# Sigmoid attention and mixture of depths: choosing rows by scatters into zeroed tables in place of selection matmuls

## Chip, cores, metric
One core of a Trainium2 chip, one launch. The metric is the device time in microseconds, here the median of three runs. All times below are in us unless marked ns.

## What is computed
An attention with a sigmoid in place of a softmax over 8 sequences, 12 heads, 448 tokens of 64 values. Its output, laid out as 8 x 448 x 768, goes into a mixture of depths: each token has a score (its dot product with w_gate); in each sequence the 128 tokens with the highest score pass through a two-layer network with a gated residual, all others are copied.

```
scores = (q @ k.T) / sqrt(64) - log(448)
x      = (sigmoid(scores) @ v)            # -> (B, S, H*64)
gate   = x @ w_gate                        # (B, S)
out    = x.copy()
for b in range(B):
    top = argpartition(-gate[b], 128)[:128]
    y   = relu(x[b, top] @ w1) @ w2        # 768 -> 1024 -> 768
    out[b, top] = x[b, top] + sigmoid(gate[b, top])[:, None] * y
```

## The kernel before
**Steps and slots.** Two quads of four heads make a step `s` (0 to 11), and a step has seven slots `n`. In each slot PE makes the scores of one 64-key piece for both quads (`score`, L339), ACT squashes them (`squash`, L353), and PE multiplies earlier pieces with v (`value`, L368). All attention matmuls use 32x64 tiles of the PE array. The value matmuls run behind the scores: those of step `s` begin in slot 4 of step `s` and end in slot 3 of step `s+1`. After slot 3 DVE takes the finished outputs out of PSUM (`takes`, four transposes at L389, into `x_b`), the loads and transposes of the next quads follow (`turn`), and the scores of the mixture's gate are made (`gates`, L397 to L431). Program order is written out by hand; each engine runs its own instructions in that order.

**PSUM.** Eight banks: `PA[0]` and `PA[1]` have two banks each, filled by `score` and emptied by `squash`; `PO[x][pr]` are four single banks, which hold the outputs of quad `x` and are emptied by `take`.

**Blocks.** From step 4 on, slot 3 is followed by a block (`block`, L680): a list of 128x128 matmul groups of the mixture, `BLOCKS[s]`. An entry `(1, p, key)` is a partial product of the first layer for the pair of sequences `p` (`first`, 24 recorded matmuls of 128 columns, L560), `(2, p, key)` of the second layer (`second`, 8 of 384 columns, L624); each pair needs seven of either kind. `("t", b)` transposes the chosen rows of sequence `b` (`turn_rows`, L524), which ACT then copies out (L526, L527), and for the second sequence of a pair DVE makes three or four differences (L533, L543). `("c", b)` chooses rows. `places` in `block` gives each entry its PSUM bank. The steps whose values precede a block (`LATE`, from the first block's step to 10) use a slot order of their own (`first_slots`, `last_slot`, `LOW`, `HIGH`), in which the outputs of quad 0 are finished before the last scores; the others use `rounds`, and the step just before `LATE` ends with a slot (`split`) in which the values of both quads finish after the scores.

**Choosing rows.** When a sequence is complete its gate scores go to DRAM and come back spread over all partitions (`spread`, L437, tile `rep`). `ranking(b)` compares every token with all others on DVE, 16 passes of 448 elements (L445, L448), and sums to each token's rank in `above + level`. `place` compares the ranks with 0..127 (`hot`, L460); for sequences 2 to 5 it also multiplies `hot` with the tokens' number and score and adds over the four columns (L469, L473). `choose` sums over the partitions with matmuls on PE: four for sequences 0, 1, 6, 7 (L486), two for 2 to 5 (L482). `fetch` turns the result into a row index (L493) and copies the score (L496), and `gather` (L506) brings the 128 rows from `out` with an indirect DMA on POOL's queue. The mixture's result is added to these rows by DVE (L635) and scattered back (`scatter`, L644, also on POOL's queue).

**Queues.** SP issues nearly all loads and stores, in order, among them the stores of `x_b` (L406), the loads of `qT`, `raw_k` and the weights; ACT issues the loads of v (`load_v`, L153) from step 5 on; POOL issues the gate scores (L425), `spread`, gathers and scatters.

Of the kernel before, what the change touches and what calls it, by code (L numbers as in the profile page):

```python
# [17 lines left out]
def kernel(  # L18
# [114 lines left out]
    def load_v(s):  # L133


        if s >= NS:
            return
        if s in (1, 3):
            t = moe.tile([P, 6 * KH * P], F32, name="rows_t")[:, :4 * NU * Dh]
        else:  # L140
            t = vals.tile([P, 4 * NU * Dh], F32, name="raw_v")
        raw_v[s] = t = t.rearrange("p (h c) -> p h c", h=4)

        def block(x, r, n):
            return bass.AP(tensor=v.tensor,
                           offset=v.offset + (8 * s + 4 * x) * S * Dh + r * Dh,
                           ap=[[TB * Dh, TT], [S * Dh, 4], [1, n * Dh]])

        for m in range(4):
            y, odd = divmod(m, 2)  # L150
            rows = slice(m * TT, (m + 1) * TT)
            if s:
                (nc.scalar if s > 4 else nc.sync).dma_start(  # L153
                    out=t[rows], in_=block(y, odd * NU, NU))
            else:
                nc.sync.dma_start(out=t[rows, :, :NA * Dh], in_=block(y, odd * NA, NA))
                nc.sync.dma_start(out=t[rows, :, NA * Dh:],
                                  in_=block(1 - y, 2 * NA + 2 * odd, 2))
# [102 lines left out]
    earlier = const.tile([P, NC, S], mybir.dt.uint8, name="earlier")  # L261

    who = [const.tile([P, NC, 2], F32, name=f"who{x}") for x in range(2)]
    slots = const.tile([P, CAP], F32, name="slots")
    above = const.tile([P, NC], F32, name="above")
    level = const.tile([P, NC], F32, name="level")
    gate_s = const.tile([P, TT], F32, name="gate_s")
    place_s = const.tile([P, NC], F32, name="place_s")
    ones = const.tile([P, 1], F32, name="ones")

    def constants():
        make_identity(nc, iden)
        for a in range(4):
            p = slice(a * TT, (a + 1) * TT)
            nc.sync.dma_start(
                out=wg_b[p],
                in_=bass.AP(tensor=moe_w_gate.tensor, offset=moe_w_gate.offset + a * TT,
                            ap=[[0, TT], [P, HP], [1, TT]]))
        nc.gpsimd.iota(slots, pattern=[[1, CAP]], base=0, channel_multiplier=0,
                       allow_small_or_imprecise_dtypes=True)  # L280

        nc.gpsimd.memset(above, float(S))
        nc.gpsimd.memset(level, 0.0)
        nc.gpsimd.memset(ones, 1.0)
# [94 lines left out]
    def takes(s, x):  # L379
        for pr in range(2):  # L380
            take(s, pr, x)
# [70 lines left out]
    def added(b):  # L452

        return 1 < b < B - 2

    def place(b):

        nc.vector.tensor_add(place_s, above, level)
# [5 lines left out]
        if not added(b):  # L464
            return

        st[b]["sums"] = both = moe.tile([P, 2, P], F32, name="sums2")
        for x in range(2):
            nc.vector.tensor_scalar(out=both[:, x, :CAP], in0=st[b]["hot"][:, 0, :CAP],  # L469
                                    scalar1=who[b % 2][:, 0, x:x + 1], scalar2=None,  # L470
                                    op0=ALU.mult)
            for c in range(1, NC):
                nc.vector.scalar_tensor_tensor(  # L473
                    out=both[:, x, :CAP], in0=st[b]["hot"][:, c, :CAP],
                    scalar=who[b % 2][:, c, x:x + 1], in1=both[:, x, :CAP],
                    op0=ALU.mult, op1=ALU.add)

    def choose(b, ps):

        if added(b):  # L480
            for x in range(2):
                nc.tensor.matmul(ps[:CAP, x:x + 1], st[b]["sums"][:, x, :CAP], ones,  # L482
                                 start=True, stop=True)
        else:
            for c in range(NC):
                nc.tensor.matmul(ps[:CAP, :2], st[b]["hot"][:, c, :CAP], who[b % 2][:, c, :],  # L486
                                 start=(c == 0), stop=(c == NC - 1))
        return b, ps

    def fetch(b, ps):  # L490
        n = CAP
        idx = moe.tile([P, 1], I32, name="idx", bufs=5)
        nc.vector.tensor_scalar(out=idx[:n], in0=ps[:n, 0:1], scalar1=float(b * S),  # L493
                                scalar2=None, op0=ALU.add)
        got = moe.tile([P, 1], F32, name="got", bufs=4)
        nc.vector.tensor_copy(got[:n], ps[:n, 1:2])  # L496
# [4 lines left out]
        st[b].update(idx=idx, xe=xe, picked=got)  # L501
        gather(b)

    def gather(b):
        n = CAP
        nc.gpsimd.indirect_dma_start(  # L506
            out=st[b]["xe"][:n], out_offset=None, in_=rows_to(b),
            in_offset=bass.IndirectOffsetOnAxis(ap=st[b]["idx"][:n, 0:1], axis=0))
# [133 lines left out]
    def scatter(b):  # L642
# [5 lines left out]


    BLOCKS = {  # L650
# [8 lines left out]
    }  # L659

    LENT = {(7, 4): [(1, 6, 2)], (8, 4): [(1, 7, 0), (1, 5, 1)],
# [17 lines left out]

    def block(s):  # L680

        places = [PA[1][:, 0], PO[0][0], PO[0][1], PA[0][:, 0], PO[1][0], PO[1][1], PA[0][:, 0]]
        work = BLOCKS.get(s, ())
        if work and work[0][0] == "c":
            chosen = choose(work[0][1], places.pop(0))
        takes(s - 1, 0)
        if work and work[0][0] == "c":
            fetch(*chosen)
            work = work[1:]
        takes(s - 1, 1)  # L690
        stores(s, NF)
        if s in FULL[::2]:
            gates(2 * s - 2)
        for item in work:
            if item[0] == "t":
                turn_rows(item[1], [places.pop(0) for _ in range(2)])
                if item[1] == 0:
                    load_v(s)
            elif item[0] == "c":
                fetch(*choose(item[1], places.pop(0)))  # L700
            else:
                finish(item, begin(item, places.pop(0)))

# [211 lines left out]
    def after(s, n):  # L915

        if n == NF and s:
            odd = s in FULL[1::2]
            if s > 5:
                load_v(s)  # L920
            elif s < 4:
                load_v(s + 1)
# [44 lines left out]
                ranking(b)  # L967
        if n != NF:
            stores(s, n)

    RANKED = [(3, 1), None, (6, 1), (7, 6), (9, 1), (10, 6), (11, 6)]

    first_outs = ExitStack()

    def stream():
# [14 lines left out]
        constants()  # L990
        for s in range(NS):
            for n in range(NU):
                if n == 0 and s:
# [39 lines left out]
```

## Time and profile before
Median 446.51 of three runs (446.19 to 446.96).

| what | value |
|---|---|
| profiled execution | 446.79, span 445.0, granted PE clock 0.997 |
| attention scores L339 | 2624 records, 242.4 busy, 537 ns each, eight tiles at a time |
| attention values L368 | 2176 + 448 + 64 records, 536 to 544 ns each |
| first layer L560 / second layer L624 | 672 records of about 276 ns / 224 records of about 487 ns |
| choose L486, L482 | 32 records of 240 to 250 ns, 16 records of 255 ns |
| DVE: hot L460 | 8, 692 ns each |
| DVE: sums L469, L473 | 8 of 284 ns, 24 of 352 ns |
| DVE: ranking L445, L448 | 64 passes, 671 to 684 ns each |
| POOL: indirect DMA | 16, about 1.0 each to issue |
| POOL: other DMA | 15, about 0.58 each to issue |

How to read it: busy times of one engine overlap, since matmuls are pipelined and lie on different parts of the array, so the mean of one matmul is longer than the distance to the next. "Idle before" names what an engine waited for. The chain that ended last shows which work set the end. A timeline row gives the start, the length, the engine, the line, output and inputs, a count where several are merged, and in brackets how long the engine had been idle and what released it.

### The profile page before, as it was taken

The numbers are of one execution on the slowest core, as the hardware profiler recorded it, in microseconds if no ns is written. First come the engines' busy times: TensorE is split into PE (matmuls) and PEld (weight loads), VectorE is DVE, ScalarE is ACT, GpSimd is POOL, SyncE is SP. The second block draws the span as 40 slices with busy tenths as digits, with TensorE's granted clock in tenths as the row PEclk, the third lists the DMA queues.
The fourth block names the chain that finished last, engine by engine and source line by source line (L and its number), as shares of the span: only waits on it lengthen the run. The fifth ranks groups of instructions, "written<-read, shape, count | busy, mean of one in ns | idle before, by whom it ended". The sixth has DMA issues, their size and how long they took to land.

```text
span 445.0 us, 14349 instructions
## 1 busy us (share of the span) xinstructions
PE 430.2 (97%) x6374; PEld 259.2 (58%) x6374; DVE 302.6 (68%) x639; ACT 191.2 (43%) x257; POOL 32.8 (7%) x55
## 2 busy tenths in 40 slices
PE   7999999999999999999999999999999999999994
PEld 3456554444457568455447559546545749769952
DVE  4316368964958986966997885835796669883462
ACT  4666666666654633641660670552363330101100
POOL 7000000000001000100002000010000101001001
PEclk9999999999999999999999999999999999999998
DMA  8984835999645997699656598499945964611001
GB/s 234 246 249 110 300 87 114 212 186 232 200 143 120 233 308 186 181 234 298 219 181 177 154 234 147 138 224 241 269 167 107 190 219 63 119 36 72 1 0 71
DMA packets 112846, 76.80 MB, mean 173 GB/s; under 512 B 90304, under 2 KB 99136, under 8 KB 112784
## 3 DMA queue, kind: packets, MB, share of 16 engines
q1 hardware_dynamic: 106768, 61.55, 53.7%
q0 software_dynamic: 1984, 7.91, 6.2%
q10 hardware_dynamic: 4032, 6.42, 6.1%
q8 instruction: 50, 0.82, 0.8%
q14 instruction: 12, 0.10, 0.1%
HBM read 55.41 MB, written 20.46 MB: 170 GB/s over the span
## 4 chain that ended last, share of the span: by engine, by line
PE 88%; DVE 5%; ACT 3%; issue 1%; DMA 1%; POOLq 0%; ACTq 0%; DVEq 0%
PE a L339 27%; PE o L368 25%; PE o L624 12%; PE o L560 10%; PE a L560 7%; PE a L624 4%; ACT attn L353 2%; PE p L989 1%; DVE spare L208 1%; PE p L339 1%; DMA out_dram<-xe,idx 1%; ACT hidden L353 1%; DVE scr L448 1%; DVE scr L445 1%; DVE scr L397 1%
## 5 line engine op out<-in xcount | busy, mean ns | idle before, releaser
L339 PE MATMUL a<-qT,kT 32*64 32x448 f32 x2624 | 242.4, 537 | 0.6 <-DVE got L496 0.5
L353 ACT ACTIVATE attn<-a,bias_s 128x896 f32<-128x896 f32 x162 | 161.4, 1007 | 83.8 <-PE a L339 79.8
L368 PE MATMUL o<-attn,raw_v 32*64 32x448 f32 x2176 | 194.6, 536 | 0.5 <-issue 0.4
L339 PEld LDWEIGHTS a<-qT,kT 32*64 32x64 f32 x2624 | 92.8, 131 | 87.1 <-ACT attn L353 49.2
L368 PEld LDWEIGHTS o<-attn,raw_v 32*64 32x64 f32 x2176 | 74.3, 131 | 35.0 <-issue 26.9
L389 DVE STREAM_TRANSPOSE x_b<-o 128x448 f32<-128x448 f32 x48 | 27.8, 623 | 46.7 <-PE o L368 26.8
L368 PE MATMUL o<-attn,rows_t 32*64 32x448 f32 x448 | 42.3, 537 | 0.2 <-issue 0.2
L576 ACT ACTIVATE hidden<-hidden 128x512 f32<-128x512 f32 x12 | 7.5, 630 | 68.5 <-DVE hidden L573 68.5
L400 DVE TENSOR_REDUCE gate_p<-scr 128x14 f32<-128x448 f32 x48 | 29.8, 622 | 1.7
L321 DVE STREAM_TRANSPOSE kT<-raw_k 128x448 f32<-128x448 f32 x42 | 24.1, 613 | 8.8 <-DMA raw_k<-in_k_dram 7.6
L397 DVE TENSOR_TENSOR scr<-x_b,wg_b 128x448 f32<-128x448 f32 x48 | 29.4, 612 | 1.1
L573 DVE TENSOR_TENSOR hidden<-o,hidden 128x512 f32<-128x512 f32 x20 | 13.3, 688 | 21.1 <-PE o L560 20.9
L624 PE MATMUL o<-w_sb,hidden 128*128 128x384 f32 x80 | 27.4, 487 | 0.0
L635 DVE SCALAR_TENSOR_TENSOR xe<-o,gate,xe 128x384 f32<-128x384 f32 x36 | 20.5, 612 | 9.5 <-PE o L624 9.3
L313 DVE STREAM_TRANSPOSE qT<-qT 128x896 f32<-128x896 f32 x23 | 25.0, 1085 | 2.1 <-DMA qT<-in_q_dram 1.9
L448 DVE SCALAR_TENSOR_TENSOR scr<-rep,who,earlier 128x448 f32<-128x448 f32 (+1 forms) x32 | 21.8, 683 | 1.4
L560 PE MATMUL o<-rows_t,w_sb 128*128 128x128 f32 x192 | 22.7, 275 | 0.0
L560 PEld LDWEIGHTS o<-rows_t,w_sb 128*128 128x128 f32 x192 | 22.2, 192 | 0.3
L526 ACT ACTIVATE rows_t<-o 128x384 f32<-128x384 f32 x7 | 3.4, 484 | 43.9 <-PE o L524 43.9
L445 DVE TENSOR_SCALAR_CACHE_REDUCE scr<-rep,who 128x448 f32<-128x448 f32 (+1 forms) x32 | 21.5, 673 | 1.0
L368 PEld LDWEIGHTS o<-attn,rows_t 32*64 32x64 f32 x448 | 17.6, 131 | 6.4 <-issue 4.7
L624 PEld LDWEIGHTS o<-w_sb,hidden 128*128 128x128 f32 x80 | 14.7, 190 | 8.8
(114 smaller groups left out, 398.1 us busy)
## 6 DMA issues: line engine op xcount, KB each, us to landing
qT<-in_q_dram SPq DMA_DIRECT2D x24, 448.0 KB, 6.0
out_dram<-x_b SPq DMA_DIRECT2D x32, 336.0 KB, 8.8
raw_k<-in_k_dram SPq DMA_DIRECT2D x22, 448.0 KB, 5.1
spare<-sum SPq DMA_DIRECT2D x18, 384.0 KB, 5.7
raw_v<-in_v_dram ACTq DMA_DIRECT2D x28, 224.0 KB, 6.1
sum<-spare SPq DMA_DIRECT2D x8, 768.0 KB, 8.3
w_sb<-in_moe_w_dram SPq DMA_DIRECT2D x6, 768.0 KB, 7.1
rows_t<-in_v_dram SPq DMA_DIRECT2D x8, 224.0 KB, 5.1
```

The lines of the kernel that those rows point to most:

```text
L313: nc.vector.transpose(heads["q", i], heads["q", i])
L321: nc.vector.transpose(kt[:, e], t[:, e].rearrange("p (a n) d -> p n a d", a=2))
L339: nc.tensor.matmul(out[y * Dh:(y + 1) * Dh, h % 2, :S], kt[d, e, r:r + 2].rearrange("d r t -> d (r t)"), qt[d, e], start=(e == 0), stop=(e ...
L353: nc.scalar.activation(a, psc[:, :, :S], AF.Sigmoid, bias=bias_s, scale=QK_SCALE)
L368: nc.tensor.matmul(PO[x][pr][j * Dh:(j + 1) * Dh, :S], raw_v[s][rows, 2 * pr + j, at:at + Dh], attn[s, pr, n][rows, j, :], start=((s, x, p ...
L389: nc.vector.transpose(x_tiles[b][:, :, 2 * g + pr, :], PO[x][pr][:, :S].rearrange("p (r t) -> p r t", t=TT))
L397: nc.vector.tensor_tensor(out=tmp, in0=x_tiles[b][:, :, hp, :], in1=wg_b[:, hp:hp + 1, :].to_broadcast([P, TB, TT]), op=ALU.mult)
L400: nc.vector.tensor_reduce(out=gate_parts[b][:, :, hp], in_=tmp, axis=AX.X, op=ALU.add)
L445: nc.vector.tensor_scalar(out=junk[:n], in0=rep[:n], scalar1=own, scalar2=0.0, op0=ALU.is_gt, op1=ALU.add, accum_out=above[:n, c:c + 1])
L448: nc.vector.scalar_tensor_tensor(out=junk[:n], in0=rep[:n], scalar=own, in1=earlier[:n, c, :], op0=ALU.is_equal, op1=ALU.mult, accum_out=l ...
L560: nc.tensor.matmul(ps[:, f, :n], w((t * FH + f) * P, P), x[:, t, :n], start=(t == 0), stop=(t == KH - 1))
L624: nc.tensor.matmul(ps[:n, :DH], h[:, t, :n], w(t * DH, DH), start=(t == 0), stop=(t == FH - 1))
```

## The change
- For sequences 0 to 5 `choose` goes. Four tables per sequence in DRAM (448 rows of 2 floats each; 24 tables) have their first 128 rows set to zero at the start by 24 DMAs on POOL's queue, from a zeroed tile. `place` scatters, for each of the four columns of tokens, the pair (number, score) to the row that is the token's rank (four indirect DMAs), then loads the first 128 rows of each table (four DMAs). Each rank below 128 is found in one of the four tables, and zero in the others; `fetch` adds the four on DVE (a reduction) and makes the index. Sequences 6 and 7 keep the matmuls; the sums at L469 and L473 and the tile `ones` go.
- `fetch` moves out of the blocks, to slots named in `FETCHED`.
- The block of step 4 goes (it held only `("c", 0)`), so `LATE` begins with step 5, and step 4 has the order of steps 1 to 3. The transposes `("t", b)` of sequences 1 to 4 move: t1 from the end of block 5 to the front of block 6, t2 from the end of block 7 to its second place, t3 from the end of block 8 to the front of block 9, t4 from the end of block 10 to its second place, t5 stays at the end of block 11.
- `places` begins with the low banks `PO[0]` in place of `PA[1]`.
- `load_v(5)` moves from ACT's queue to SP's, `load_v(6)` and `load_v(9)` go behind the transposes in their block. `ranking` of sequences 3 and 5 comes one slot earlier.

```diff
-                (nc.scalar if s > 4 else nc.sync).dma_start(
+                (nc.scalar if s > 5 else nc.sync).dma_start(
...
+    tables = [[dram.tile([S, 2], F32, name=f"table{b}_{c}", bufs=1) for c in range(NC)]
+              for b in range(B - 2)]
...
+        for t in sum(tables, []):
+            nc.gpsimd.dma_start(out=t[:CAP].rearrange("i x -> (i x)"), in_=zero[0:1, :2 * CAP])
...
     def place(b):
+        if b < B - 2:
+            rank_of = moe.tile([P, NC], I32, name="rank_of")
+            nc.vector.tensor_add(rank_of, above, level)
+            for c, n in enumerate(HELD):
+                nc.gpsimd.indirect_dma_start(
+                    out=tables[b][c][:, :], in_=who[b % 2][:n, c], in_offset=None,
+                    out_offset=bass.IndirectOffsetOnAxis(ap=rank_of[:n, c:c + 1], axis=0))
+            st[b]["rows"] = rows = moe.tile([P, NC, 2], F32, name="rows", bufs=2)
+            for c in range(NC):
+                nc.gpsimd.dma_start(out=rows[:CAP, c], in_=tables[b][c][:CAP])
+            return
...
-    def fetch(b, ps):
+    def fetch(b, ps=None):
...
+        got = moe.tile([P, 2], F32, name="got", bufs=5)
+        if b < B - 2:
+            nc.vector.tensor_reduce(out=got[:n], in_=st[b]["rows"][:n].rearrange("p c x -> p x c"),
+                                    axis=AX.X, op=ALU.add)
+        else:
+            nc.vector.tensor_copy(got[:n], ps[:n, 0:2])
+        nc.vector.tensor_scalar(out=idx[:n], in0=got[:n, 0:1], scalar1=float(b * S),
                                 scalar2=None, op0=ALU.add)
...
-        4: [("c", 0)],
-        5: [("c", 1), ("t", 0), (1, 0, 1), (1, 0, 2), ("t", 1)],
-        6: [(1, 0, 6), ("c", 2), (2, 0, 1), (1, 0, 7), (1, 0, 4), (1, 0, 5)],
-        7: [(1, 0, 3), (2, 0, 2), (2, 0, 5), (2, 0, 6), (2, 0, 3), ("t", 2)],
-        8: [("c", 3), (2, 0, 4), (2, 0, 7), (1, 1, 1), (1, 1, 2), ("t", 3)],
-        9: [("c", 4), (1, 1, 6), (2, 1, 1), (1, 1, 7), (1, 1, 4), (1, 1, 5)],
-        10: [(1, 1, 3), (2, 1, 2), (2, 1, 5), (2, 1, 6), (2, 1, 3), ("t", 4)],
-        11: [("c", 5), (2, 1, 4), (2, 1, 7), (1, 2, 1), (1, 2, 2), ("t", 5)],
+        5: [("t", 0), (1, 0, 1), (1, 0, 2)],
+        6: [("t", 1), (2, 0, 1), (1, 0, 6), (1, 0, 7), (1, 0, 4), (1, 0, 5)],
+        7: [(1, 0, 3), ("t", 2), (2, 0, 2), (2, 0, 5), (2, 0, 6), (2, 0, 3)],
+        8: [(2, 0, 4), (2, 0, 7), (1, 1, 1), (1, 1, 2)],
+        9: [("t", 3), (2, 1, 1), (1, 1, 6), (1, 1, 7), (1, 1, 4), (1, 1, 5)],
+        10: [(1, 1, 3), ("t", 4), (2, 1, 2), (2, 1, 5), (2, 1, 6), (2, 1, 3)],
+        11: [(2, 1, 4), (2, 1, 7), (1, 2, 1), (1, 2, 2), ("t", 5)],
...
-        places = [PA[1][:, 0], PO[0][0], PO[0][1], PA[0][:, 0], PO[1][0], PO[1][1], PA[0][:, 0]]
+        places = [PO[0][0], PO[0][1], PA[1][:, 0], PA[0][:, 0], PO[1][0], PO[1][1], PO[1][0]]
...
-                if item[1] == 0:
+                if s in (6, 9):
                     load_v(s)
...
-            if s > 5:
+            if s > 4 and s not in (6, 9):
                 load_v(s)
...
+        if (s, n) in FETCHED:
+            fetch(FETCHED[s, n])
...
-    RANKED = [(3, 1), None, (6, 1), (7, 6), (9, 1), (10, 6), (11, 6)]
+    RANKED = [(3, 1), None, (6, 1), (7, 5), (9, 1), (10, 5), (11, 6)]
+    FETCHED = {(4, 0): 0, (5, 5): 1, (6, 5): 2, (8, 4): 3, (9, 5): 4, (11, 1): 5}
```

More of the change, by code (lines that the diff above doesn't have):

```diff
@@ L268, with constants @@
     place_s = const.tile([P, NC], F32, name="place_s")
-    ones = const.tile([P, 1], F32, name="ones")
-    def constants():
+    def constants(zero):
         make_identity(nc, iden)
@@ L283, in constants @@
         nc.gpsimd.memset(level, 0.0)
-        nc.gpsimd.memset(ones, 1.0)
+        for t in sum(tables, []):
+            nc.gpsimd.dma_start(out=t[:CAP].rearrange("i x -> (i x)"), in_=zero[0:1, :2 * CAP])
         for t in (gate_s, *who):
@@ L450, in rank @@
             op0=ALU.is_equal, op1=ALU.mult, accum_out=level[:n, c:c + 1])
-    def added(b):
-        return 1 < b < B - 2
     def place(b):
+        if b < B - 2:
[9 more added lines that the diff above has]
+            return
         nc.vector.tensor_add(place_s, above, level)
@@ L463, in place, with gather @@
             in1=place_s.rearrange("p (c o) -> p c o", o=1).to_broadcast([P, NC, CAP]))
[L464 to L476, printed above, removed]
-    def choose(b, ps):
[L480 to L487, printed above, removed]
+    def choose(b, ps):
+        for c in range(NC):
+            nc.tensor.matmul(ps[:CAP, :2], st[b]["hot"][:, c, :CAP], who[b % 2][:, c, :],
+                             start=(c == 0), stop=(c == NC - 1))
         return b, ps
-    def fetch(b, ps):
+    def fetch(b, ps=None):
         n = CAP
         idx = moe.tile([P, 1], I32, name="idx", bufs=5)
-        nc.vector.tensor_scalar(out=idx[:n], in0=ps[:n, 0:1], scalar1=float(b * S),
+        got = moe.tile([P, 2], F32, name="got", bufs=5)
[5 more added lines that the diff above has]
+        nc.vector.tensor_scalar(out=idx[:n], in0=got[:n, 0:1], scalar1=float(b * S),
                                 scalar2=None, op0=ALU.add)
-        got = moe.tile([P, 1], F32, name="got", bufs=4)
-        nc.vector.tensor_copy(got[:n], ps[:n, 1:2])
+        st[b].update(idx=idx, picked=got[:, 1:2])
+        gather(b)
+    def gather(b):
+        n = CAP
         if b == B - 1:
@@ L500, in fetch @@
             xe = moe.tile([P, D], F32, name="xe", bufs=3)
[L501 to L505, printed above, removed]
+        st[b]["xe"] = xe
         nc.gpsimd.indirect_dma_start(
@@ L680, in block @@
     def block(s):
-        places = [PA[1][:, 0], PO[0][0], PO[0][1], PA[0][:, 0], PO[1][0], PO[1][1], PA[0][:, 0]]
[L683 to L690, printed above, removed]
+        places = [PO[0][0], PO[0][1], PA[1][:, 0], PA[0][:, 0], PO[1][0], PO[1][1], PO[1][0]]
+        for x in range(2):
+            takes(s - 1, x)
         stores(s, NF)
@@ L693, in block @@
             gates(2 * s - 2)
-        for item in work:
+        for item in BLOCKS[s]:
             if item[0] == "t":
                 turn_rows(item[1], [places.pop(0) for _ in range(2)])
-                if item[1] == 0:
+                if s in (6, 9):
                     load_v(s)
-            elif item[0] == "c":
-                fetch(*choose(item[1], places.pop(0)))
             else:
@@ L989, in stream @@
             nc.tensor.matmul(outs[1][:, 0], zero[:, :P], zero, start=True, stop=True)
-        constants()
+        constants(zero)
         for s in range(NS):
```

## Prediction
> **What bounds the kernel now.** I read the page first: engine totals, the chain that ended last, the groups. Then the timeline at the entry of every block (a block is the batch of expert matmuls in slot 3 of a step), the DVE row of the timeline between blocks, and POOL's own instructions.
>
> ```profile
> span 445.0 us, 14349 instructions
> PE 430.2 (97%) x6374; PEld 259.2 (58%) x6374; DVE 302.6 (68%) x639; ACT 191.2 (43%) x257; POOL 32.8 (7%) x55
> PE 88%; DVE 5%; ACT 3%; issue 1%; DMA 1%; POOLq 0%; ACTq 0%; DVEq 0%
> ```
>
> TensorE carries 88% of the chain. So a matmul taken away counts in full, a DVE instruction only where PE waits for it, and POOL is nearly free. The rest is in the seams, where PE goes from attention to a block and back:
>
> ```profile
> 105.22 0.93 PE L368 MATMUL o<-attn,rows_t 32*64 32x448 f32 x8
> 106.08 1.05 PE L486 MATMUL a<-who,hot 128*128 128x2 f32 x8
> ...
> 230.62 0.55 PE L339 MATMUL a<-qT,kT 32*64 32x448 f32 x4
> 230.67 0.35 DVE L473 SCALAR_TENSOR_TENSOR sums<-hot,who,sums 128x128 f32<-128x128 f32 x1
> 230.93 1.17 DVE L321 STREAM_TRANSPOSE kT<-raw_k 128x448 f32<-128x448 f32 x2
> 231.53 0.60 PE L482 MATMUL a<-ones,sums 128*128 128x1 f32 x4 [0.35 <-ACT attn L353]
> 232.02 1.14 DVE L389 STREAM_TRANSPOSE x_b<-o 128x448 f32<-128x448 f32 x2
> 232.69 0.59 PE L624 MATMUL o<-spare,hidden 128*128 128x384 f32 x1 [0.56 <-DVE x_b L389]
> ```
>
> In block 4 PE changes over 0.07 us before the modelled end of the last attention matmul (105.22+0.93=106.15): that is the price of the change-over when the bank is free. In block 8 (and 6, 7, 9, 10, 11: 0.30 to 0.44 of wait) it stands until ACT has squashed the high bank PA[1]. Block 8 waits a second time: DVE was still ranking and adding the table up, so its takes (x_b) came late.
>
> **The change, part by part.**
>
> *Matmuls gone.* The choose of sequences 0 to 5: 8+8+4+4+4+4=32 records. They follow each other at 0.112 us (8 from 106.08, the next kind at 130.22 after 129.34: 0.88/8=0.11). Each part below includes its own.
>
> *Steps 4 and 5.* Step 4 loses its block and runs as steps 2 and 3 do. From first matmul of slot 5 to the same a step later: 41.27, 63.59, 86.42, 110.64, so 22.3 and 22.8 for the plain steps, 24.2 with block 4. A stall inside slot 1 (a gap of 0.7 at 96.66, released by nothing shown) should stay, so I take 22.9 for the new step: gain 1.3. Step 5 then gets the slot order that step 4 had: from slot 5 to the last attention matmul 18.6 (19.2 less that stall) instead of 17.7, a loss of 0.85. Its block opens with the transposes of sequence 0 in PO[0], which in that order finishes last: the first take started 0.16 after 106.08, lasts 0.6, then 1.1 from first transpose to first matmul (130.22 to 131.33). That is 2.55 after the last attention matmul instead of 2.98 with choose: gain 0.4. The exit of block 5 no longer ends on copies in PA[0] (slot 4 takes 3.6 us after blocks 5 and 8, 3.05 after 6, 7, 9, 10): gain 0.5. Together 1.4, bounds 0.5 and 2.4.
>
> *Block 6:* choose 0.45, change-over 0.37: 0.8. DVE had run into it with the adds of sequence 2 (until 162.28); without them the takes start near 158.8. The transposes of sequence 1 now come first; the next matmul on their differences follows (2,0,1), which covers copies and three subtractions by a few tenths. Uncovered, these cost up to 1.
>
> *Block 7 and 10:* change-over from PA[1] to PO[0][0], whose take is done in time (x_b 194.59 and 301.55): 0.5 each.
>
> *Block 8:* DVE drops hot (0.69), two L469 (0.28) and six L473 (0.35): 3.4 us, and adds one 0.16. Its takes then wait for PE alone, and (2,0,4) starts at 231.1 instead of 232.69: 1.6. The exit as in block 5: 0.5. Ranking moved one slot earlier passes nothing: DVE is busy without a break and no other work lies between.
>
> *Block 9:* choose 0.45 and change-over 0.35: 0.8.
>
> *The tables themselves.* Per sequence POOL issues 4 scatters and 4 loads; DVE adds a reduce of 0.24 (as L415) and keeps idx (0.16). POOL is idle over 90%, so its 6.3 us are covered, six times. What is not plain is the latency, because fetch now stands in DVE's queue:
>
> ```profile
> L506 POOL DMA_INDIRECT xe<-out_dram,idx x7: 974/997/1052, 107.7 to 377.1; - x7
> L425 POOL DMA_DIRECT2D scores<-total x8: 530/568/777, 66.1 to 375.9; - x8
> DMA to landing us min/median/max: 1.6/2.4/5.4
> DMA to landing us min/median/max: 3.0/4.0/7.1
> ```
>
> (The third line is that of L425, 1.8 KB; the fourth that of L644, 384 KB scatters.) Chain: POOL starts 0.2 after the ranks, four issues of 1.0, the last lands 1.8 after its issue ends (2.4-0.57, the small transfer), 0.1, a load of 2.4, then reduce, idx and hand-overs 0.5: 9.0 us from the ranks. For sequences 0 to 4 DVE reaches fetch 15 to 31 us after the ranks (81.6 to 96.4; 120 to 150; 159 to 188; 227 to 252; 261 to 293), so nothing waits. Their gathers (longest 8.0) land before the transposes; the closest is sequence 2, issued near 188.8, landed by 197, wanted at 198. Should it miss, up to 1 us. On POOL gather 2 now stands ahead of spread(3), which left at 187.8 and leaves 1 to 2 us later; its rows are first read at 221. No other spread or row scatter queued behind a table or gather is wanted sooner.
>
> Sequence 5 is different: ranking after slot (10,5), fetch after (11,1), and nothing between them on DVE, which is behind anyway:
>
> ```profile
> 331.25 0.16 DVE L458 TENSOR_TENSOR place_s<-above,level 128x4 f32<-128x4 f32 x1
> 333.86 1.13 DVE L473 SCALAR_TENSOR_TENSOR sums<-hot,who,sums 128x128 f32<-128x128 f32 x3
> 337.12 1.18 DVE L389 STREAM_TRANSPOSE x_b<-o 128x448 f32<-128x448 f32 x2 [2.14 <-PE o L368]
> ...
> 339.30 0.57 PE L624 MATMUL o<-kT,hidden 128*128 128x384 f32 x1
> ```
>
> Ranks at 331.4, table read and summed at 340.4, but the takes of step 11 were ready at 337.1. They stand behind the reduce in DVE's queue, and block 11 now opens on PO[0][0], which wants the first of them: 340.5+0.65+0.1=341.25 against 339.30 now. Loss 1.95. Both small landings at their shortest (1.6): 339.55, loss 0.25. Scatter at 7.1 and load at 5.4: 348.4, loss 9.1. I take the median of the 1.8 KB row, the nearest in size. Behind it gather 5 leaves at 341 and is wanted at 351: covered.
>
> [...]
>
> *Loads moved.* load_v(5) goes to SP, idle from 124.8 to 143: nothing. load_v(6) and (9) go behind the transposes' copies on ACT: 2 us later, landing 6 to 8 us on, some 2 us before slot 4 wants them. If that cover fails, 1 us each.
>
> *Start.* 24 zeroing DMAs on POOL, 0.57 each, in the first 16 us, beside loads that hold the DMA engines at 0.87 of their time. POOL's other constants are wanted at 60 us. I take 0.2 lost; bounds 0 and 1.
>
> **Sum:** 1.4+0.8+0.5+2.1+0.8+0.5 = 6.1 gained; block 11 loses 1.95 and regains 0.1 at its exit; start 0.2. Net 4.05. The profiled execution took 446.79 (span 445.0 and 1.8 around it), 0.28 above the median of the runs, 446.51. So 442.5.
>
> **Rivals.**
> - *Short landings.* Small transfers on a quiet queue land in 1.6 (two of the eight did in 1.7); block 11 loses 0.3, all else holds: 440.8. Against it: eight back to back.
> - *The change-over is not free.* 0.07 rests on one seam that also left a different slot order. If PE always needs the 0.9 us that the other six seams show from the start of the last matmul, 2.1 of the gains go: 444.6.
> - *Table latency on the path (the slower side).* Place: DVE's wait in front of the takes of block 11. Price: a microsecond of total time for each microsecond of chain. With landings of 7.1 and 5.4 it costs 7.2 more than forecast: 449.6. It decides once the chain exceeds 9+4.05=13 us from the ranks. For it: stores make small transfers slow (4.7 and 5.4 were seen among the scores), 768 KB x2 of loads are issued at 326 to 329. Against: the DMA engines are only 0.55 busy from 330 to 345.
> - *The change doesn't do what it says:* zeroing, four tables with one hit per rank, and the sum give the same index; nothing speaks for this.
>
> **How the numbers follow.** About 0.2% (0.9 us) is what a measurement of this kernel can tell from no change. Forecast 0.47; short landings 0.17; change-over 0.16; table latency 0.20, of which 0.14 ends above 447.4 and 0.06 between. With tails of the others 0.02 more falls within 0.2%. Faster 0.78, same 0.08, slower 0.14. The likeliest case alone spans 441 to 444; the range reaches to the ends of the other cases, 439.6 to 447.2.
>
> **What would show it.** No L486 or L482 before 360 us; block entries 6 to 10 without a wait on ACT; (2,0,4) of block 8 released by PE's own order; in block 11 DVE idle before the reduce for some 8 us, released by a table load, and PE waiting for x_b behind it. I am wrong if DVE waits at an earlier fetch, if transposes wait for a gather, or if block 11 starts later than 5 us after its last attention matmul.

## Result and the profile after
The changed kernel took 450.64 (median of 450.54 to 452.67, four runs); the kernel before 446.56 (446.19 to 446.96, four runs). The ratio is 1.0102 [1.0072, 1.0132]: slower by 1%, above the range forecast. The profiled execution took 450.7. On another chip the same kernel lost 5% (run 16 below).

The page of the kernel after: span, engine totals, the chain that ended last, and the new scatters among the groups.

```profile
span 448.7 us, 14346 instructions
...
PE 428.0 (95%) x6342; PEld 256.0 (57%) x6342; DVE 289.4 (64%) x601; ACT 191.1 (43%) x257; POOL 83.8 (19%) x126
...
PE 88%; DVE 4%; ACT 2%; DMA 2%; issue 2%; POOL 1%; POOLq 0%; DVEq 0%; ACTq 0%
...
L460 POOL DMA_INDIRECT table<-who,rank_of x24 | 23.5, 980 | 85.6 <-DVE rank_of L458 80.1
```

The 32 matmul records are gone from PE and 13 us from DVE, as the change says. In the chain "DMA" and "issue" have grown by one point each: PE waits somewhere for a table, and something at the end waits for nothing shown.

I compared the start of each slot's first attention matmul in the two profiles. Up to slot (11,3) after gains 9.13. From (11,3) to (11,4), that is through block 11, it needs 23.25 in place of 15.38: 7.87 lost. At the last matmul it is still 1.41 ahead (437.04 against 438.44). Then the end takes 5.1 longer, and the span is 3.7 longer. Two places, then.

**Block 11.** POOL's row of the timeline (start, length, engine, line, operation, output and inputs, count, in brackets the idle time before and its releaser):

```profile
323.22 0.98 POOL L460 DMA_INDIRECT table<-who,rank_of  x1 [13.13 <-DVE rank_of L458]
324.50 0.96 POOL L460 DMA_INDIRECT table<-who,rank_of  x1 [0.30 <-issue]
325.76 0.92 POOL L460 DMA_INDIRECT table<-who,rank_of  x1 [0.30 <-issue]
326.99 0.91 POOL L460 DMA_INDIRECT table<-who,rank_of  x1 [0.30 <-issue]
327.89 0.58 POOL L465 DMA_DIRECT2D rows<-table  x1
329.07 1.61 POOL L465 DMA_DIRECT2D rows<-table  x3 [0.59 <-DMA table<-who,rank_of]
```

DVE's row at the same place:

```profile
322.77 0.16 DVE L458 TENSOR_TENSOR rank_of<-above,level 128x4 int32<-128x4 f32 x1
...
334.36 0.16 DVE L486 TENSOR_REDUCE got<-rows 128x2 f32<-128x8 f32 x1 [11.43 <-DMA rows<-table]
...
334.64 2.24 DVE L391 STREAM_TRANSPOSE x_b<-o 128x448 f32<-128x448 f32 x4
```

And the windows of five microseconds (busy time and count of PE, PE's weight loads, DVE, ACT, POOL; then the granted PE clock, the share of the DMA engines, GB/s):

```profile
325.00:330.00 5.00, 4.35 (x96) 1.89 (x80) 0.00 (x0) 3.60 (x6) 3.80 (x6) 1.00 0.04 4
330.00:335.00 5.00, 0.00 (x0) 0.00 (x0) 0.60 (x3) 0.55 (x1) 0.69 (x2) 0.89 0.91 182
335.00:340.00 5.00, 4.66 (x8) 2.54 (x9) 4.79 (x11) 0.00 (x0) 0.98 (x1) 0.50 0.60 125
340.00:345.00 5.00, 5.00 (x26) 3.64 (x25) 3.60 (x13) 0.00 (x0) 0.65 (x2) 0.92 0.98 150
```

The wait is where the prediction put it: DVE stands before the reduce for 11.43, released by a table's load, with the takes behind it and PE behind those. From the ranks to the reduce it is 11.6, not 9.0. The scatters follow each other at 1.27, since 0.3 passes after each. The last load is issued at 330.15, 0.96 after the last scatter landed, because the loads are issued one after the other (at 329.07, 329.63 and 330.15), and DVE goes on 4.2 after that issue began; from 330 to 335 the DMA engines are at 0.91. PE has no matmul from 330 to 335, and then the last column but two falls to 0.50: the clock is halved from 333.95 for 6.83 us, so that the first eight records of the block follow each other at 0.64 instead of 0.32. Block 11 starts 6.5 after its last attention matmul did, later than the 5 that the prediction named as a sign of being wrong.

**The end.** When its work is done, each engine ends with an instruction DRAIN. POOL's, by its line (shortest, median and longest in ns, first and last start), and SP's, before:

```profile
L1028 POOLq DRAIN  x3: 40/102/4597, 439.6 to 444.7; - x3
L1028 SPq DRAIN  x3: 7/7/7, 443.5 to 444.5; - x3
```

and after:

```profile
L1018 POOLq DRAIN  x3: 40/102/9688, 438.2 to 448.4; - x3
L1018 SPq DRAIN  x3: 7/7/7, 442.0 to 448.2; - x3
```

The last transfer has landed when SP drains, at 443.5 in before and 442.0 now. POOL's drain, which starts at 438.2, goes on for 9.69 in place of 4.60: to 447.9, with no DMA packet after 442, where in before it outlasts SP's by 0.7. POOL's queue had 31 transfers before and has 103 now.

### The profile page after: what moved, and what is told of

Read it like the earlier page. It is cut to its first block, busy times and chain, and to the rows that moved or that the text cites. A ratio compares the mean times of both kernels' runs of the same rounds, so it can differ in the third digit from the quotient of the medians.

```text
span 448.7 us, 14346 instructions
## 1 busy us (share of the span) xinstructions
PE 428.0 (95%) x6342; PEld 256.0 (57%) x6342; DVE 289.4 (64%) x601; ACT 191.1 (43%) x257; POOL 83.8 (19%) x126
## 4 chain that ended last, share of the span: by engine, by line
PE 88%; DVE 4%; ACT 2%; DMA 2%; issue 2%; POOL 1%; POOLq 0%; DVEq 0%; ACTq 0%
PE a L341 26%; PE o L370 26%; PE o L620 11%; PE o L556 10%; PE a L556 7%; PE a L620 5%; PE p L979 1%; PE o L520 1%; DMA rows<-table 1%; ACT attn L355 1%; POOL table L460 1%; ACT hidden L355 1%; DMA out_dram<-xe,idx 1%; DVE scr L447 1%; DVE gate_p L402 1%
## 5 line engine op out<-in xcount | busy, mean ns | idle before, releaser
L460 POOL DMA_INDIRECT table<-who,rank_of x24 | 23.5, 980 | 85.6 <-DVE rank_of L458 80.1
L569 DVE TENSOR_TENSOR hidden<-o,hidden 128x512 f32<-128x512 f32 x22 | 14.4, 687 | 21.9 <-PE o L556 21.8
L556 PE MATMUL o<-rows_t,spare 128*128 128x128 f32 x216 | 25.7, 276 | 0.7 <-DVE x_b L391 0.7
L556 PEld LDWEIGHTS o<-rows_t,spare 128*128 128x128 f32 x216 | 24.7, 192 | 2.9 <-DVE x_b L391 2.9
L631 DVE SCALAR_TENSOR_TENSOR xe<-o,gate,xe 128x384 f32<-128x384 f32 x32 | 18.3, 611 | 11.4 <-PE o L620 11.2
L427 POOL DMA_DIRECT2D scores<-total x8 | 4.5, 558 | 111.9 <-DVE by_token L429 111.9
L620 PE MATMUL o<-spare,hidden 128*128 128x384 f32 x72 | 24.4, 489 | 0.0
L640 POOL DMA_INDIRECT out_dram<-xe,idx x7 | 7.0, 999 | 78.0 <-DVE xe L631 74.9
```

The costliest lines, as they stand in the source:

```text
L460: nc.gpsimd.indirect_dma_start(out=tables[b][c][:, :], in_=who[b % 2][:n, c], in_offset=None, out_offset=bass.IndirectOffsetOnAxis(ap=rank ...
L556: nc.tensor.matmul(ps[:, f, :n], w((t * FH + f) * P, P), x[:, t, :n], start=(t == 0), stop=(t == KH - 1))
L620: nc.tensor.matmul(ps[:n, :DH], h[:, t, :n], w(t * DH, DH), start=(t == 0), stop=(t == FH - 1))
```

## The experiments
**1 and 2: block 11.** The first moves `fetch(5)` behind the takes, the second makes the ranks earlier.

```diff
             takes(s - 1, x)
+        if s == 11:
+            fetch(5)
...
-    FETCHED = {(4, 0): 0, (5, 5): 1, (6, 5): 2, (8, 4): 3, (9, 5): 4, (11, 1): 5}
+    FETCHED = {(4, 0): 0, (5, 5): 1, (6, 5): 2, (8, 4): 3, (9, 5): 4}
```
```diff
+            if s == 10:
+                ranking(5)
             if s not in FULL[::2]:
                 gates(2 * s - 2)
...
-    RANKED = [(3, 1), None, (6, 1), (7, 5), (9, 1), (10, 5), (11, 6)]
+    RANKED = [(3, 1), None, (6, 1), (7, 5), (9, 1), None, (11, 6)]
```

> fetch of sequence 5 moved from slot (11,1) to block 11, behind the four takes. Theory W (the loss is DVE's wait in front of the takes, PE's half clock after it, and a longer drain of POOL at the end): PE's gap before block 11 falls from 6.5 to about 0.5 us, the granted clock stays at 1.0, block 11 then waits up to 1 us for its transposes (the gather leaves at 335) and up to 1 us at its exit; POOL's drain stays at 9.7: 443 to 445 us. Rival M (the latency of the tables is on the path wherever fetch stands): the transposes wait instead of the takes, 448 to 451.

> ranking of sequence 5 moved ahead of gates(18) and gates(19) in step 10, 5.1 us earlier on DVE; fetch stays at (11,1). Theory W: the tables are read before the takes of step 11 are ready (about 328) or less than 1 us after, no half clock, drain 9.7 unchanged: 441.5 to 443. Rival M: POOL or the DMA engines, not DVE's order, set when the tables come: the wait stays at 4 us or more, 447 or more.

Measured: 445.02, ratio 0.9955 [0.9927, 0.9983], and **442.97**, ratio 0.9912 [0.9882, 0.9943]. The stretch is 16.38 and 14.65, the clock stays at 1.0 in both, the drain is 9.69 in both. DVE in the second:

```profile
318.56 0.16 DVE L458 TENSOR_TENSOR rank_of<-above,level 128x4 int32<-128x4 f32 x1
...
329.49 0.16 DVE L486 TENSOR_REDUCE got<-rows 128x2 f32<-128x8 f32 x1 [5.63 <-DMA rows<-table]
...
329.77 2.24 DVE L391 STREAM_TRANSPOSE x_b<-o 128x448 f32<-128x448 f32 x4
```

The chain is hardly shorter (10.9), but it starts 4.2 earlier, and the takes come when the values are ready. The second kernel beats before on this chip, and by itself the late block 11 was worth more than the whole loss.

**3: zeroing on SP's queue.** The 24 zeroing transfers of the kernel after leave POOL for SP.

```diff
-        for t in sum(tables, []):
-            nc.gpsimd.dma_start(out=t[:CAP].rearrange("i x -> (i x)"), in_=zero[0:1, :2 * CAP])
...
+        if (s, n) == (1, 0):
+            for t in sum(tables, []):
+                nc.sync.dma_start(out=t[:CAP].rearrange("i x -> (i x)"), in_=blank[0:1, :2 * CAP])
```

> The 24 zeroing DMAs leave POOL's queue for SP's, in slot (1,0); the stall in block 11 stays. Theory W1 (POOL's last drain costs about 0.07 us for each DMA it has issued: 31 before, 4.6 us; 103 after, 9.7 us): drain 8.0, total 448.9. Rival W2 (it goes by packets, 384 of the 2304 added are theirs): drain 8.9, total 449.8. Rival W3 (it waits for the last scatter or for something else): drain 9.7, total 450.6. The start may move by up to 0.5 either way.

Measured: 448.93, ratio 1.0059 [1.0036, 1.0081]; the drain is 7.73 with 79 transfers on POOL's queue, 0.3 below what W1 said. The late block 11 is still there.

**4 and 5: wait and clock apart.** Matmuls that nobody reads, at the head of block 11, keep PE busy while it waits: 48, and 25 in the fifth run.

```diff
+        if s == 11:
+            for _ in range(48):
+                nc.tensor.matmul(PA[1][:, 0, :P], w1_sb[:, 0, :P], iden, start=True, stop=True)
```

> 48 matmuls of 128x128x128 whose result nobody reads are put on PE at the head of block 11, into PA[1], so that PE is busy during the wait (5.4 us of 6.4). Theory W: the granted clock stays at 1.0 through block 11, (2,1,4) and (2,1,7) take 1.29 us per four matmuls instead of 2.7, total 448.0. Rival C (the clock falls for another reason, or the wait alone is the loss): clock 0.5 at the same place, total 450.6.

> The changed kernel with 25 instead of 48 unread matmuls at the head of block 11: each is recorded twice, 0.112 us apiece, so 5.6 us of PE work, less than the wait. Theory W (half clock after the wait is part of the loss): clock 1.0 through block 11, 448.0. Rival C (only the wait is the loss): 450.6 at an unchanged wait even with the clock at 1.0.

Measured: 453.93, ratio 1.0161 [1.0122, 1.02], and 449.26, ratio 1.008 [1.005, 1.011]. 48 were too many: they lasted 10.8, longer than the wait, and the stretch grew to 25.65. With 25 (5.6 us) the windows of the same place read:

```profile
330.00:335.00 5.00, 4.65 (x53) 4.14 (x38) 0.00 (x0) 1.71 (x2) 1.62 (x3) 1.00 0.65 140
335.00:340.00 5.00, 5.00 (x27) 3.67 (x26) 4.34 (x10) 0.00 (x0) 0.98 (x1) 1.00 0.57 128
```

The clock is 1.00 throughout, PE works at 27 matmuls in place of 8 from 335 to 340, and the stretch is 20.58. The wait is the same: in both runs DVE's reduce starts 7.47 after the slot's first score matmul. So the halved clock alone costs 23.25-20.58=2.67, and the wait 20.58-14.65=5.9. (The profiled executions differ by 1.48 only, as this one is 1.16 later before block 11.)

**6 and 7: two parts undone, each in the kernel of run 2.** The bank order of before, and the empty block of step 4.

```diff
-        places = [PO[0][0], PO[0][1], PA[1][:, 0], PA[0][:, 0], PO[1][0], PO[1][1], PO[1][0]]
+        places = [PA[1][:, 0], PO[0][0], PO[0][1], PA[0][:, 0], PO[1][0], PO[1][1], PA[0][:, 0]]
```
```diff
     BLOCKS = {
+        4: [],
         5: [("t", 0), (1, 0, 1), (1, 0, 2)],
```

> e2_rank_early with the bank order of before (PA[1] first in every block). By the prediction's sum each of the entries of blocks 6 to 11 waits 0.35 to 0.5 us for ACT again, block 5's copies come up to 0.8 earlier: 1 to 2.5 us over e2, 444 to 445.5. Rival: the change of banks is worth nothing, 443.0.

> e2_rank_early with an empty block back in step 4, so that steps 3 and 4 have the slot order of before but no choose. By the prediction's terms (step 4 gains 0.4 beside its choose, step 5 loses 0.85, and block 5 opens 0.9 later than it could) the block's absence costs: 441.7. Rival: taking the block away is itself a gain: 444 to 445.

Measured: 446.64, ratio 1.0007 [0.9981, 1.0032], and 444.03, ratio 0.9941 [0.9908, 0.9973]. High banks first costs 0.36 to 0.44 at each entry of blocks 6 to 10, as predicted, and another 0.6 at the exits of 6 and 9, which were not in my sum: low banks first is worth some 3. The empty block of step 4 shows no difference up to block 5, so the expectation that leaving it out costs 1.3 fails. In slots (6,4) and (6,5) run 7 loses 1.4; there a weight load waits 0.9 for the loads of v, issued up to 4 us later than in run 2. Its profiled execution is the slowest of ten, and the intervals of runs 2 and 7 overlap. Without block 4 nothing, or up to 1, is gained.

**8: fewer transfers, one table per sequence.** All 448 ranks differ, so scatters that follow each other need only one table, with nothing zeroed and nothing summed; sequence 5, which is in a hurry, keeps four.

```diff
-    tables = [[dram.tile([S, 2], F32, name=f"table{b}_{c}", bufs=1) for c in range(NC)]
-              for b in range(B - 2)]
+    ALONE = 5
+    tables = [[dram.tile([S, 2], F32, name=f"table{b}_{c}", bufs=1)
+               for c in range(NC if b == ALONE else 1)] for b in range(B - 2)]
...
-                    out=tables[b][c][:, :], in_=who[b % 2][:n, c], in_offset=None,
+                    out=tables[b][c % len(tables[b])][:, :], in_=who[b % 2][:n, c], in_offset=None,
...
+        if b < B - 2 and b != ALONE:
+            got = st[b]["rows"][:, 0]
```

> e2_rank_early with one table in place of four for sequences 0 to 4 (all 448 ranks differ, so every row is written once; the four scatters follow one another, nothing is zeroed or summed) and four zeroed ones for sequence 5 alone: 68 DMAs on POOL's queue instead of 103. Theory W1 (POOL's last drain goes by the number of DMAs, about 0.07 us each): drain 7.1 to 7.3, total 440.5. Rival W2 (by packets; the scatters keep theirs): drain 8.5 or more, 441.8 or more. Rival: the serial scatters (about 4 us each) make DVE wait at a fetch and the takes come late: 443 or more.

Measured: 446.39, ratio 0.9997 [0.9968, 1.0027]; drain 6.83 with 68 transfers, 0.3 below what W1 said, as in run 3. But the chain of sequence 0 became 26 long, `fetch(0)` at (4,0) stood in front of the takes, and PE idled 3.42 and then ran at half clock (0.50 for 6.83): 6.5 lost there.

**9 and 11: sequence 0 gets its four tables back,** in the kernel of run 8, once with zeroing on POOL's queue and once on SP's.

```diff
-    ALONE = 5
+    APART = (0, 5)
```

> e8_one_table, but sequence 0, whose serial scatters made block 4's place wait, has four zeroed tables again, as sequence 5: 75 DMAs on POOL's queue. Theory W: no wait for a table anywhere but the few tenths of e2, clock at 1.0 throughout, drain 7.2 to 7.5, total 440.7 (e2 less 2.3). Rival: another fetch waits (sequence 1 to 4): a half clock and 446 or more again.

> e9_two_apart with its eight zeroing DMAs on SP's queue in slot (1,0): 67 on POOL's queue. Drain 0.5 to 0.7 shorter than e9, total 440.1; if SP's queue is held up in step 1, up to 1 us more than that.

Measured: 453.11, ratio 1.0144 [1.0106, 1.0181], and 451.4, ratio 1.0122 [1.0076, 1.0168]. The drains are 7.40 and 6.75 as expected; the times are 12 and 11 off. New stalls of 3.3 at slot (3,4) and 2.8 to 3.6 at (11,0) stand where the scatters of sequences 0 and 5 are under way. Runs 13 to 18 follow this up.

**10 and 12: the drain by itself.** To the kernel before I added transfers on POOL's queue in slot (1,0) that nobody reads: 72 of 1 KB (the diff), and 12 of 384 KB.

```diff
+        if (s, n) == (1, 0):
+            for t in unread:
+                nc.gpsimd.dma_start(out=t.rearrange("i x -> (i x)"), in_=blank[0:1, :2 * CAP])
```

> The kernel before with 72 more DMAs of 1 KB on POOL's queue in step 1, which nobody reads and nothing waits for. Theory W1/W2 (the last drain pays for each): drain 9.5 to 10.5, total 451.5. Rival W3 (the drain was long for another reason, such as the tables or the last scatter): drain 4.6, total 446.4.

> The kernel before with 12 more DMAs of 384 KB (80 packets each by the last scatter's record, against 32 of a small one) on POOL's queue in step 1. W1 (the drain goes by DMAs, 0.07 to 0.08 each): drain 5.5. W2 (by packets, 2.2 ns each): drain 6.7. The loads beside them may be late by a few us, so the drain is read and not the total.

Measured: 452.17, ratio 1.0123 [1.0086, 1.0161], and 452.98, ratio 1.0142 [1.0092, 1.0191]. The drain of before with 72 more transfers:

```profile
L1034 POOLq DRAIN  x3: 40/102/9702, 438.0 to 448.3; - x3
```

Before plus 72 transfers has the drain of after to 0.02, and of the 5.95 that it loses the drain is 5.1. The 12 large ones have 112 packets each instead of 32 and add only 0.48 (5.08). That is below what either expectation said, 5.5 by number and 6.7 by packets, and nearer to the number. Over all kernels: 31 transfers 4.60, 43 5.08, 64 6.50, 67 6.75, 68 6.83, 75 7.40, 79 7.73, 103 9.69: 0.08 for each from 64 on, and 0.06 on average from 31 to 64. Why the first ones cost less is not shown. (The time of the run with large ones holds another loss: loads came late at 24 to 28, and PE stood.)

**13 and 14: do the cures add up, and what are the new stalls?** Runs 2 and 3 joined; and run 9 with all 24 tables held in DRAM, so that each engine has the same instructions with the same waits and only addresses differ.

> The kernel after with both edits that helped: ranking of sequence 5 ahead of the last gates of step 10, and the 24 zeroing DMAs on SP's queue in slot (1,0). Theory W (the loss of the kernel after is made of a late block 11 and of POOL's last drain, and the two are independent): 442.97 with the first edit alone; the drain falls from 9.69 to 7.7 (79 DMAs on POOL's queue), of which the second edit gave back 1.7 by itself: 441.2, clock 1.0 throughout. Rival X (in these kernels a rare stall of PE without a releaser falls where it will as soon as anything is moved, as in the two kernels with one table): some 443 to 452, with drain 7.7 all the same.

> The kernel with one table for sequences 1 to 4 and four for 0 and 5 (453.11), all 24 tables held in DRAM again, those not used left unread: each engine has the same instructions with the same waits, only addresses in DRAM differ. Theory P (the stalls of 3.2 at (3,4) and 2.8 at (11,0) hang on where the program's data or code lie in DRAM): they go or move, and the time falls towards 441 to 447. Rival Q (they come from the instructions themselves, such as what POOL issues beside the scatters): they stay in the same slots, 453.

Measured: **467.93**, ratio 1.05 [1.0458, 1.0541], and 453.92, ratio 1.0154 [1.0121, 1.0188]. The addresses change nothing: slot (3,4) lasts 6.57 against 6.47, and 3.18 in run 2. The joined kernel has stalls of 3 to 4 beside nearly every set of scatters. Runs 1 to 8 had been on two chips without any such stall; runs 9, 11, 13 and 14, all that had them, were on two others.

**15, 16 and 17: the same kernels on another chip.** Runs 2, after and 13 again, unchanged, all on one chip.

> The kernel with ranking of sequence 5 early once more, unchanged (442.97 before). In the first 6 us after the first scatter of a sequence PE started 115 to 128 attention matmuls in the runs of the first nine kernels, and 53 to 60 in those of the four kernels that stalled, which all ran on two other chips. Theory Y (beside the four scatters PE runs at half its rate on some chips): where this run falls on such a chip, it starts 53 to 60 after the scatters of sequences 0 and 5 and takes 449 to 466, with before at 446.3 beside it; on another chip 443. Rival Q (the stalls belong to the four kernels): 443 and 115 to 128 wherever it runs.

> The kernel after once more, unchanged (450.64 before). Theory Y: on a chip that slows PE beside scatters 457 to 475, else 450.6. Rival Q: 450.6 on any chip.

> Ranking early and zeroing on SP's queue once more, unchanged (467.93 before). Theory Y: on a chip that slows PE beside scatters 466 to 470, else 441.2, with a drain of 7.7 on either. Rival Q: 468 on any chip.

Measured: 469.54, ratio 1.0513 [1.0472, 1.0555]; **469.52**, ratio 1.05 [1.0472, 1.0528]; 469.62, ratio 1.0484 [1.0444, 1.0523]; before 446.95 beside them. The kernel of run 2 took 442.97 on one chip and 469.54 on this. Four microseconds in which the scatters of sequence 0 are issued, run 2:

```profile
82.00:86.00 4.00, 4.00 (x92) 2.59 (x80) 3.71 (x6) 2.75 (x3) 3.09 (x4) 1.00 0.98 248
```

The same kernel, the same window, on this chip:

```profile
82.00:86.00 4.00, 4.00 (x52) 1.36 (x39) 1.18 (x2) 1.01 (x1) 3.08 (x4) 1.00 0.99 249
```

PE has 52 matmuls in work in place of 92, at a granted clock of 1.00, the same DMA share and the same four scatters. What its engines wait for from 82 to 92 there (us in total, times, longest):

```profile
ACT attn L355 <- remote: 5.0, 1, 5.0
DVE x_b L391 <- remote: 3.4, 1, 3.4
PEld o L370 <- issue: 2.8, 6, 0.8
PEld a L341 <- issue: 2.1, 4, 1.2
```

For ACT and DVE the profile names no releaser ("remote"); by the program, what they read there are PE's results. PE's own weight loads wait for "issue", that is for nothing that the profile shows.

So rival Q falls. But each chip was used in one stretch of time, and the two without stalls came first. Whether it is the chip, or something that changed between the runs, is not separated.

**18: scatters one after the other, on the chip of 15 to 17.** One table for sequences 0 to 4, two zeroed tables for sequence 5, `fetch(0)` later, `fetch(5)` behind the takes of block 11 (the diff is against run 8).

```diff
-               for c in range(NC if b == ALONE else 1)] for b in range(B - 2)]
+               for c in range(2 if b == ALONE else 1)] for b in range(B - 2)]
...
             takes(s - 1, x)
+        if s == 11:
+            fetch(5)
...
-    FETCHED = {(4, 0): 0, (5, 5): 1, (6, 5): 2, (8, 4): 3, (9, 5): 4, (11, 1): 5}
+    FETCHED = {(4, 6): 0, (5, 5): 1, (6, 5): 2, (8, 4): 3, (9, 5): 4}
```

> Ranking of sequence 5 early; one table for each of sequences 0 to 4, its four scatters one after the other (all 448 ranks differ, so every row is written once; nothing is zeroed or summed); two zeroed tables for sequence 5; fetch(0) moved from slot (4,0) to (4,6), fetch(5) behind the takes in block 11. 64 transfers on POOL's queue. Theory Y (on some chips PE runs at half its rate while four scatters are under way at once, not beside scatters that follow each other: in the kernels with one table for sequences 1 to 4 the stalls stood at sequences 0 and 5 alone): no stall at sequences 0 to 4 on any chip; 115 to 128 matmuls started in the 6 us after their first scatter where PE is in attention; at sequence 5, with two under way, at most half of the 4.3 lost on such a chip. Drain 6.6. Time 442.97 less 3.1 for the drain: 440 on a chip without the stalls, 440 to 442.5 on one with them, below before's 446.4 on either. Rival Z (any scatter of 8-byte rows slows PE there): on such a chip each of the six costs 3 to 5 again, 455 to 470.

Measured: 458.93, ratio 1.0305 [1.0266, 1.0344], drain 6.50. The same window:

```profile
82.00:86.00 4.00, 4.00 (x91) 2.48 (x79) 3.38 (x7) 2.57 (x3) 0.86 (x1) 1.00 1.13 194
```

91 matmuls: the stall at sequence 0 is gone (slot (3,4) lasts 3.44, against 8.63 in run 15 and 3.18 in run 2). Sequences 2 and 3 lose 0.42 and 0.15 at their scatters against 3.72 and 3.58. With two tables for sequence 5, 1.41 are lost against 4.27. So scatters that wait for each other cost little, and Z falls. What it is about four in a row isn't settled: run 18 spaces POOL's issues as well as the transfers. In run 15 PE is slow before any packet of POOL's queue has moved (the first at 84.9; POOL issues from 82.0). Run 2 and then run 15:

```profile
84.00:84.90 0.90, 0.90 (x30) 0.62 (x21) 0.90 (x3) 0.55 (x1) 0.59 (x2) 1.00 1.36 219
84.00:84.90 0.90, 0.90 (x11) 0.27 (x7) 0.00 (x0) 0.00 (x0) 0.60 (x2) 1.00 1.36 228
```

So the slowing begins before the scatters' data move. Nor does any issue back to back bring it: run 10, on a chip with stalls, issues 21 plain transfers one behind the other from 31.8 to 42, and each slot is as long as in before. Back-to-back indirect issues on POOL fit what is seen; no run tests them alone.

The time is off for a reason of my own making, in POOL's queue:

```profile
130.68 0.96 POOL L461 DMA_INDIRECT table<-who,rank_of  x1 [4.97 <-DMA table<-who,rank_of]
135.03 0.58 POOL L466 DMA_DIRECT2D rows<-table  x1 [3.39 <-DMA table<-who,rank_of]
136.01 0.99 POOL L505 DMA_INDIRECT xe<-out_dram,idx  x1 [0.40 <-issue]
```

The moved `fetch(0)` issues its gather behind the scatters of sequence 1, which now wait for each other from 118 to 135. PE stood 12.05 for `xe` and then ran at half clock (0.50 for 13.65); slot (5,4) starts 12.3 late. Without that 446.6 would be left, still not 440 to 442.5: there are further steps of 0.4 to 0.6 at six slots, 2.9 together. Four of them, at (7,4), (8,6), (10,1) and (10,4), stand in runs 9 and 15 too, far from any table scatter. In each of these slots POOL issues one gather or one scatter of chosen rows. In run 2 they have their usual length of 3.0 to 3.1; so do (7,4) and (10,4) in run 10, the kernel before on a chip with stalls, where POOL issues the same row scatters. So rows of 8 bytes are no condition for these steps, and why before is spared stays open.

## Why the prediction was wrong
- *"POOL is nearly free"* was the step that failed by itself. POOL's issue time was indeed covered, but the transfers on its queue make the drain at the end longer, and there nothing covers it: 72 transfers, 5.1. No term of the sum and no rival had it, and 442.5+5.1 is already above the range. Run 10 shows it with nothing else of the change. The prediction took the end of before, with its drain of 4.6, as it stood, and never asked what its length depends on.
- *The tables' chain for sequence 5* had the right place, the right order of waits, and the wrong size: 11.6 for 9.0. Issues at 1.0 became 1.27, the last load was issued 0.96 after the last scatter's landing for 0.1, and it took 4.2 for 2.4. `load_v(11)` on ACT's queue ran just then (DMA share 0.91 from 330 to 335); in run 2, where the last load comes before `load_v(11)`, it takes 1.9. The prediction's "0.55 busy from 330 to 345" was read from before, where those loads are issued from 338.75 on. Without the halved clock block 11 costs 20.58-15.38=5.2 where 1.95 was forecast: 2.6 from the chain, and 0.65 because up to there DVE's ranks had gained 8.48 and PE 9.13.
- *The halved clock* (2.67) was missing. Where PE stood for 3.42 (run 8), 6.0 (after) and 12.05 (run 18), the granted clock fell to 0.50 for 6.83, 6.83 and 13.65 us. What sets these lengths was not shown. Forecasting 1.95 of further wait, I never asked how long PE would stand in all.
- *Rival "table latency on the path"* was the right mechanism with a price of a microsecond for each microsecond; the clock made it dearer (2.67 on top of a wait of 5.9). Its deciding point, a chain of 13, wasn't reached; the drain used up the margin first.
- *The gains* were right in kind and somewhat too small: 6.1 forecast, 9.13 measured up to (11,3). Of this 0.55 is a different start, and some 1.6 are two stalls in the profiled execution of before (gaps of 0.71 at 96 and 0.97 at 296), the first of which I took to stay. Runs 10 and 12, which have the blocks of before, have neither; against run 10 after gains 7.1, the start taken off. Block 8 brought 2.9 (2.1), steps 4 and 5 with block 5 2.9 (1.4; 2.2 against run 10), blocks 7 and 10 0.48 each (0.5 each). Blocks 6 and 9 brought less, 0.44 and 0.27 (0.8 each). In blocks 6 to 10 of after PE changes over 0.07 before the modelled end of the last attention matmul, as forecast, so the rival "the change-over is not free" falls; run 6 confirms the price. I left out what the bank order does at the exits. Leaving out block 4 gains 1.3 up to slot (5,3), beside its choose, and loses 1.2 in block 5 (run 7 against run 2); by the prediction's terms it was 0.4 and 1.75.
- *Sequences 0 to 4* wait for nothing in the first measurement, as forecast: no fetch and no transposes there stand for a table. On the chips with stalls PE was slow beside nearly every set of four scatters in a row (run 15: 52 matmuls in 4 us; run 2: 92); nothing in the trace of before could show that.
- 4.05 net gain was forecast, and the span grew by 3.7. Block 11 cost 7.9 (1.95 forecast) and the end 5.1 (nothing forecast). With block 11 cured and the drain still paid, the change is a gain of 0.9% (run 2). Whether curing the drain as well adds to that was not seen: the joined kernel ran only on chips where the scatters' stalls cover it.

## What to carry to other kernels
Before moving work to an idle queue, look at the end of the program: if that engine's last drain is what finishes, each transfer has a price (here 5.1 for 72), however well its issue is hidden. When a wait on PE grows, add up how long PE stands in all and price the clock after it (here 2.67 after PE stood for 6.0). And repeat a close comparison on another chip and at another time: one change was 1% slower here and 5% there, and its best variant 0.9% faster here and 5% slower there.

## What the hardware showed
- POOL's closing drain: 4.60 with 31 transfers, 6.50 with 64, 9.69 with 103. 72 small transfers with nothing else of the change give 9.70; 12 large ones of 112 packets each add 0.48.
- Indirect transfers back to back on POOL: 1.27 apart, 0.3 of it between them.
- A wait of PE of 6.0 cost another 2.67 by a halved clock (6.83 at 0.50); with unread matmuls in the wait the clock stayed at 1.00.
- In the runs on three of five chips, PE at about half its rate beside four back-to-back indirect scatters (52 against 92 matmuls in work in 4 us, clock 1.00), and hardly slowed beside scatters that wait for each other. Before took 446.0 to 447.0 on all five. How POOL's transfers reach PE, and why only there, stays open; different addresses in DRAM made no difference.
